# Operand building moved in among the weight-gradient tiles, and dq with ds stationary, in a decode step's backward pass

## The chip, the cores and the metric

One core of a Trainium2 chip runs one program: the forward and backward pass of a four-layer decode step for one token. The metric is the device time of one execution, in microseconds (us). The core has a matrix engine (TensorE, PE in the profile), a vector engine (VectorE, DVE), a scalar engine (ScalarE, ACT) and GpSimd (POOL), each with its own instruction queue; SyncE (SP) only issues transfers here. SBUF is the on-chip memory, PSUM the memory that TensorE writes to, and 16 DMA engines move data to and from device memory (HBM).

## What is computed

The reference runs x = x + A(LN(x)); x = x + B(LN(x)) twice (layers A1, B2, A3, B4) with shared weights, and returns the output and the gradients of all inputs:

```python
def _A_ref(x, k_cache, v_cache, wq, wo):          # x: 1x1x1024, Hq=32, Hkv=4, Dh=128
    W = min(4096, max(256, Sk // 4))              # 4096 of 32768 cached positions
    q = (x @ wq).reshape(B, Sq, Hq, Dh).transpose(0, 2, 1, 3)
    k = jnp.repeat(k_cache[:, :, Sk - W:, :], rep, axis=1)
    v = jnp.repeat(v_cache[:, :, Sk - W:, :], rep, axis=1)
    p = softmax(einsum("bhqd,bhkd->bhqk", q, k) * Dh ** -0.5)
    o = einsum("bhqk,bhkd->bhqd", p, v)
    return o.transpose(0, 2, 1, 3).reshape(B, Sq, Hq * Dh) @ wo
def _B_ref(x, w1, b1, w2):                        # F = 3584
    h = einsum("bsd,df->bsf", x, w1) + b1
    act = h * tanh(softplus(h))                   # mish
    return einsum("bsf,fd->bsd", act, w2)
```

There is one token, so each weight's gradient is a sum of two outer products (one for each layer that uses the weight), and the gradients of the two caches are zero outside the last 4096 positions. Those zeros and the weight gradients are most of what is written.

## The kernel before

All matrix-vector work of one layer is staged behind the loads of its weights. `wq` (`wq_b`), K, V and ten of the sixteen `wo` pieces (`wo_b`) stay in SBUF; w1, w2 and the other six `wo` pieces are loaded again for each pass, in pieces of 448 or 512 KB, into six stream buffers. The order is attention A1 forward, MLP B2 forward, A3 forward, B4 forward and backward in one, `attn_bwd` of A3 (there `first` is true), MLP B2 backward, `attn_bwd` of A1, and then the tail: all weight gradients and the gradients of K and V.

The transfers of zeros (112 of 512 KB) are issued in small groups from POOL's queue (`bg_zeros`, L134) beside the passes, and what is left, 27 of them, from SP's queue in one go (`zeros`, L128) after the last loads of A1's pass. SP's queue is in order: the last `wo` loads, these zeros, a reload of p (L905, `area["p3"]`), then the stores of the tail.

`attn_bwd` (L803) goes through these steps. `T` (L817) transposes a late `wo` piece on TensorE, has it evacuated by ScalarE, and reduces its other half on VectorE; `M` (L826) multiplies. A row pass over the kept `wo` (`drow`) gives the rest of do. `do_p` collects do, two small transposes and products spread it (`dps`, `qps`), and `rows_mm` (L416) computes d = do V^T into two halves `hv` with 32 products, four at a time in column groups of 32. VectorE forms the row sums of p*d (L922) and ds = p*(d - sum) (L933). `half_T` (L431) transposes ds to `dsT`. `cols_mm` (L423) computes dq with 128 products: K is the stationary operand, and 8 columns of `dsT` move. ScalarE scales the result to `dq_bf` (L947). The pass over `wq` (L951) takes 64 products of one broadcast column by 512 into four row strips, `rows_copy` (L242) copies them to SBUF, `rows_sel2` (L251) folds the strips with four fp32 products, and `ln_bwd` (L305) finishes the layer. `warm(n)` (L151) issues n products that nobody reads, between steps. In the A3 pass `fill` (L271) transposes pieces of K, V and wq back beside these steps.

The weight gradients need their operands as rows. These are made by small builds, kept as closures in the list `prep` and issued one at a time by `nextprep` (L1141) at places written by hand inside A1's `attn_bwd`. `spread_rows` (L977: `rows_put`, `tall_left`, `tall_right`) has POOL scatter columns into one of two spread tiles, TensorE transpose up to eight blocks, and ScalarE evacuate them. `row_layout` (L395) takes four products and four masked copies on VectorE (L401). `db1_out` (L1215) writes the gradient of b1.

The tail is a list of jobs, one for each output chunk of [128, 2048] (or 1792), run in order: 14 chunks of dw2 (`dw_tall`), 16 of dw1 (`dw_wide`), 8 of dV (`dkv`), 16 of dwo, 8 of dK, 16 of dwq. A job takes two PSUM tiles of two banks each from the pool `pair` (four such tiles, all of PSUM), fills them with four outer products (eight for dV and dK), evacuates one half at a time, and issues a store from SP; `dkv` stores only after every fourth chunk, two transfers of 1 MB. `ev_out` gives a half to VectorE or ScalarE, whichever has the smaller sum of costs (`evac`, L143: 1.22 against 1.05 a half); other work of VectorE is not counted there.

Of the kernel before, what the change touches and what calls it, by code (L numbers as in the profile page):

```python
# [8 lines left out]
FP32 = mybir.dt.float32  # L9
# [5 lines left out]
P = 128  # L15
HQ = 32
DH = 128
G = 4
# [5 lines left out]
def kernel(  # L24
# [126 lines left out]
    def warm(n):  # L151

        ps = psum1([P, 4, P], FP32, "wps")
        for _ in range(n):
            nc.tensor.matmul(ps, lhsT=ident_bf[:], rhs=ident_bf[:, None, :].to_broadcast([P, 4, P]),  # L155
                             start=True, stop=True, skip_group_check=True)

    def shaped(t, shape):
        n = 1
        for k in shape[1:]:  # L160
            n *= k
        ap = t[0:shape[0], 0:n]
        if len(shape) == 3:
            return ap.rearrange("p (a b) -> p a b", a=shape[1])
        if len(shape) == 4:
            return ap.rearrange("p (a b c) -> p a b c", a=shape[1], b=shape[2])
        return ap

    def psum1(shape, dtype, name):
        return shaped(pt.tile([P, 512 if dtype == FP32 else 1024], dtype, name=name, tag="pt"), shape)  # L170

    def top(kind):
# [12 lines left out]
    def xpose(blocks, dst, how=None, six=False):  # L185

        n = len(blocks)
        pools["turn"] += 1
        if six and pools["turn"] % 6 > 3:
            ps = shaped(pools["top"].tile([P, 1024], BF16, name="tps", tag="h"), [P, 8, P])  # L190
        else:
            ps = psum1([P, 8, P], BF16, "tps")
        for b, ap in enumerate(blocks):
            nc.tensor.transpose(ps[:, b, :], ap, ident_bf[:])  # L194
        evac(dst, ps[:, 0:n, :].rearrange("p b c -> p (b c)"), 0.08 * n + 0.05, 0.11 * n + 0.15, how)

    def nat_blocks(ap2d, nb=8):
        return [ap2d[:, b * P:(b + 1) * P] for b in range(nb)], ap2d
# [106 lines left out]
    def ln_bwd(dn_ps, n32, rstd, g_col, name, nxt):  # L305

        tt = work.tile([P, 2 * TD], FP32, name="tt")
        nc.vector.tensor_copy(tt[:, 0:TD], dn_ps)
        nc.vector.tensor_mul(tt[:, TD:], tt[:, 0:TD], n32[:])
        sps = sm_tile(P, 2 * TD)  # L310
        nc.tensor.matmul(sps[:], lhsT=onesD, rhs=tt[:], start=True, stop=True)
        if nxt == "A1":
            warm(7)
        if nxt == "B2":
            hook("ln")
        ab = work.tile([P, 2], FP32, name="ab")
        nc.vector.reduce_sum(ab[:], sps[:].rearrange("p (a b) -> p a b", a=2), axis=AX.X)
        t2 = work.tile([P, TD], FP32, name="t2")
        nc.vector.scalar_tensor_tensor(out=t2[:], in0=n32[:], scalar=ab[:, 1:2], in1=tt[:, 0:TD],
                                       op0=ALU.mult, op1=ALU.subtract, reverse1=True)  # L320
        gx = work.tile([P, TD], FP32, name="gx")
        nc.vector.tensor_scalar(out=gx[:], in0=t2[:], scalar1=ab[:, 0:1], scalar2=rstd[:, 0:1], op0=ALU.subtract, op1=ALU.mult)
        g_new = keep.tile([P, TD], FP32, name=f"g_{name}")
        nc.vector.tensor_add(g_new[:], g_col[:], gx[:])
        g_bf = pair_col("g" + nxt[0], nxt, TD)
        nc.vector.tensor_copy(g_bf, g_new[:])
        return g_new, g_bf
# [67 lines left out]
    def row_layout(col32, name):  # L395
        x = area[name].rearrange("p (g d) -> p g d", g=G)
        ps = psum1([P, P], FP32, "rps")
        for c in range(NC):
            mm(ps[32 * c:32 * c + 32, 0:P], col32[:], ident_bf[:], True, True, tile_position=(0, 32 * c))
        for g in range(G):  # L400
            nc.vector.tensor_scalar(out=x[:, g, :], in0=ps[:, 0:P], scalar1=gmask[:, g:g + 1], scalar2=None, op0=ALU.mult)  # L401
# [401 lines left out]
    def attn_bwd(g_col, g_bf, lname, sv, first, nxt):  # L803
# [13 lines left out]
        def T(i):  # L817
            c = late[i]
            if c not in held:
                held[c] = wo_load(c)  # L820
            w = held[c]
            xpose(*nat_blocks(w[:, 1, :]), "a")
            nc.vector.tensor_tensor_reduce(out=w[:, 0, :], in0=w[:, 0, :], in1=gbc[:], scale=1.0, scalar=0.0,
                                           op0=ALU.mult, op1=ALU.add, accum_out=wdo[:, i:i + 1])

        def M(i):  # L826
            c = late[i]
# [21 lines left out]
        if not first:  # L849
            after_do()  # L850
            prep.extend([
                lambda: tall_left("w2", "a", 0),
                lambda: tall_left("w2", "a", 1),
                lambda: tall_right("w2", "gB"),
                lambda: rows_put(area["R1"], 0, "nB", "rep"),
                lambda: rows_put(area["R1"], 1, "dh", "pieces"),
                lambda: row_layout(sA3["dorep"], "do3"),
                lambda: row_layout(sA3["qrep"], "q3"),
            ])

        for i in range(2, len(late) + 1):
# [16 lines left out]
        if first:  # L878
            fill(1, ["K", "wq"], "a")
        else:  # L880
            warm(4)
        dps = psum1([HQ, P], BF16, "dps")
        nc.tensor.transpose(dps[:, 0:P], do_p[:].rearrange("p t c -> p (t c)"), ident_bf[:])
        dr = work.tile([HQ, P, 2], BF16, name="dr", tag="rw5", padded_shape=[HQ, P, 2])
# [8 lines left out]
        for e in range(2):  # L893
            mm(qps[:, :, e], drf[:, e * P:(e + 1) * P], fold16[:], e == 0, e == 1)
        if not first:
            warm(2)
        sv["dorep"] = pad_cols(pad, qps[:].rearrange("p c e -> p (c e)"), 1.0, f"do_{lname}")
        top("halves")
        hv = halves("d")
# [1 line left out]
        if first:  # L901
            fill(3, ["K", "wq"], "a")
        else:
            after_v()
            nc.sync.dma_start(area["p3"], out_5[0:P, :])  # L905
            prep.extend([
                lambda: tall_left("wo", "o", 0),
                lambda: tall_left("wo", "o", 1),
                lambda: tall_right("wo", "gA"),
                lambda: rows_put(area["Rq"], 0, "nA", "rep"),  # L910
                lambda: row_layout(sA1["dorep"], "do1"),
                lambda: row_layout(sA1["qrep"], "q1"),
                db1_out,
            ])
            nextprep(2)
            warm(3)
        scr = work.tile([P, WC], BF16, name="scr", tag="kp")
        sdp = work.tile([P, 2], FP32, name="sdp")
# [8 lines left out]
        nc.vector.tensor_copy(sd[:], lps[:])  # L927
        ds = sv["p"] if first else area["ds"]
        dsT = work.tile([P, TJ, P], BF16, name="dsT", tag="kp")
        qacc = acc_tile(HQ)  # L930
        for hf in range(2):
            hs = slice(hf * 512, (hf + 1) * 512)
            nc.vector.scalar_tensor_tensor(out=ds[:, hs], in0=hv[hf][:], scalar=sd[:, 0:1], in1=sv["p"][:, hs], op0=ALU.subtract, op1=ALU.mult)  # L933
# [1 line left out]
        if first:  # L935
            fill(100, ["K"], "a")
        else:
            nextprep(1)
            warm(3)
        for hf in range(2):  # L940
            half_T(ds, dsT, hf, "va"[hf])
        if not first:
            nextprep(1)
        for hf in range(2):
            cols_mm(qacc, dsT, kv["K"], hf)
        dq_bf = pair_col("dq", lname, HQ)
        nc.scalar.activation(dq_bf, qacc[:], ACT.Copy, scale=scale)  # L947
        if first:
# [2 lines left out]
        for h in range(HQ):  # L951
            for half in range(2):
                row_mm(nrow, 2 * half + h % 2, dq_bf[:, h:h + 1],
                       wq_b[:, 4 * half:4 * half + 4, h // 16, (h % 16) * P:(h % 16 + 1) * P], h < 2, h >= HQ - 2)
            if not first and h % 6 == 5:
                nextprep()
        nps = sm_tile(P, TD)
        yr = rows_copy(nrow, "v")
        if first:
            hook("copy")  # L960
        else:
            rows_put(area["Rq"], 1, "dq", "heads")
        rows_sel2(yr, Cols8(nps, True))
        if first:
            hook("sel")
# [11 lines left out]
    def spread_rows(n, put, dst):  # L977

        sp = area["spread"][pools["sturn"] % 2]
        pools["sturn"] += 1  # L980
        for l in range(2):
            put(sp.rearrange("p j (q x) -> p j q x", q=4), l)
        ps = psum1([P, 8, P], BF16, "rw")
        for j in range(n):
            nc.tensor.transpose(ps[:, j, :], sp[:, j, :], ident_bf[:])
        evac(dst, ps[:, 0:n, :].rearrange("p j x -> p (j x)"), 0.69, 1.0, "a")

    def rows_put(R, side, kind, how):

# [19 lines left out]
    def tall_left(nm, kind, half):  # L1009

        src = pairs[kind]
        nb = src.shape[2] // 2
        lo, n = 8 * half, min(8, nb - 8 * half)

        def put(spread, l):
            c = src[:, l, 2 * lo:2 * (lo + n)].rearrange("p (c t) -> p c t", t=2)
            for tt in range(2):
                nc.gpsimd.tensor_copy(spread[:, 0:n, 2 * tt:2 * tt + 2, l], c[:, :, tt:tt + 1].to_broadcast([P, n, 2]))

        spread_rows(n, put, tall[nm][:, lo * P:(lo + n) * P])  # L1020
# [120 lines left out]
    def nextprep(n=1):  # L1141
        for _ in range(min(n, len(prep))):
            prep.pop(0)()
# [80 lines left out]

    g0, g0b = attn_bwd(g1, g1b, "A1", sA1, False, "X0")
    level()
    nextprep(100)
    col_out(g0b, TD, out_1[0, 0, :])
    top(None)
    pacc.release()  # L1230
# [4 lines left out]
        return area[nm].rearrange("p (g d) -> p g d", g=G)  # L1235

    slots.extend(wq_t)
    dkv(area["p3"], r3("do3"), sA1["p"], r3("do1"), out_3)
    dw_tall("wo", HQ, out_5.rearrange("(c p t) d -> c p t d", p=P, t=2))
    dkv(sA3["ds"], r3("q3"), sA1["ds"], r3("q1"), out_2)  # L1240
    dw_wide(lambda: area["Rq"], 512, 2048, False, out_4)
    run(1000)
    zeros(1000)
    assert not zero_jobs
# [30 lines left out]
```

## Time and profile before

| | us |
|---|---|
| median of 8 runs | 450.67 (446.31 to 453.22) |
| the profiled execution, its own time | 451.45 |
| its span in the profile | 449.6 |
| busy PE / PEld / DVE / ACT / POOL | 325.8 / 220.5 / 235.4 / 225.0 / 63.9 |
| moved by DMA | 171.20 MB, mean 381 GB/s |
| last loads issued, last zeros issued by SP | 294.6, 330.4 |
| first evacuation of a dW chunk, its store issued | 344.65, 346.00 |

PEld is the load of a stationary operand. A row of the timeline gives the start, the length, the engine, the source line, what is written and read, the number of instructions, and in brackets how long the engine had been idle and who released it. Many rows carry L230, L194 or L149 because small helpers issue most matmuls, transposes and copies; they are told apart by the names of the tiles: `acc<-dsT,K` is dq, `acc<-wq_b,dq_pair` the pass over wq, `d` the product with V, `kps` the transposes of ds, `rw` the transposes of operand rows, `rps` the row layouts, `wps` warm-ups, `ops` the outer products of the tail.

### The profile page before, as it was taken

How to read it: one execution, taken by the hardware profiler on the slowest of the kernel's cores; microseconds unless marked ns; L12 is line 12 of the kernel's file. 1: busy time of each engine (PE TensorE's matmuls, PEld its weight loads, DVE VectorE, ACT ScalarE, POOL GpSimd, SP SyncE). 2: the span in 40 equal slices, each digit the busy share in tenths (PEclk: the TensorE clock that was granted, in tenths of full speed). 3: DMA queues.
4: the chain of work that ended last, by engine and by line, in shares of the span. 5: the costliest groups of instructions: out<-in, count | busy, mean ns of one | idle time of the engine just before them, and what ended most of it. 6: DMA issues, size and time to landing. Idle time of an engine off the chain costs nothing.

```text
span 449.6 us, 12085 instructions
## 1 busy us (share of the span) xinstructions
PE 325.8 (72%) x5180; PEld 220.5 (49%) x5180; DVE 235.4 (52%) x484; ACT 225.0 (50%) x262; POOL 63.9 (14%) x165
## 2 busy tenths in 40 slices
PE   0465856497988798977899579796775857989720
PEld 0233515496466798964897579764532111112100
DVE  3124201196333476782265765463415978999930
ACT  1122100075153486875693355427214988998930
POOL 2000000011332122251341102015001000000000
PEclk9999555576879899998799668969867555555555
DMA  8999999999999999999999999999992999899998
GB/s 318 374 414 417 407 408 375 408 367 360 405 414 374 396 330 383 368 402 417 414 414 394 361 367 343 408 393 412 414 399 82 403 404 403 334 406 400 407 406 326
DMA packets 52049, 171.20 MB, mean 381 GB/s; under 512 B 5184, under 2 KB 12380, under 8 KB 50972
## 3 DMA queue, kind: packets, MB, share of 16 engines
q1 hardware_dynamic: 39536, 125.58, 72.3%
q0 software_dynamic: 12416, 44.84, 25.2%
q8 instruction: 40, 0.66, 0.6%
q14 instruction: 13, 0.11, 0.1%
q10 hardware_dynamic: 44, 0.01, 0.0%
HBM read 71.58 MB, written 98.84 MB: 379 GB/s over the span
## 4 chain that ended last, share of the span: by engine, by line
PE 23%; ACT 15%; DMA 6%; issue 5%; DVE 3%; POOL 1%; DVEq 0%; ACTq 0%; SPq 0%; POOLq 0%
PE ops L230 7%; DMA w_c<-in_B_w_dram 6%; PE tps L194 6%; ACT wq_b L149 5%; PE acc L230 3%; ACT K L149 3%; ACT wo_b L149 2%; ACT st_o L149 2%; PE wps L155 1%; ACT V L149 1%; PE sm L230 1%; PE d L230 1%; ACT wo_c L149 1%; PE tps L628 1%; DVE K L146 1%
## 5 line engine op out<-in xcount | busy, mean ns | idle before, releaser
L139 POOL DMA_DIRECT2D out_dram<-zt x85 | 45.5, 538 | 45.5 <-DMA out_dram<-zt 40.3
L230 PEld LDWEIGHTS <-w_c 128*128 128x128 bf16 x1120 | 37.3, 102 | 22.2 <-DMA w_c<-in_B_w_dram 16.8
L638 ACT COPY w_c<-tps 128x1024 bf16<-128x1024 bf16 x28 | 28.3, 1012 | 27.1 <-PE tps L628 19.8
L652 DVE CUSTOM_DVE_ANT_0 scr<-w_c,gbc 128x1024 bf16<-128x1024 bf16 x28 | 34.2, 1221 | 9.2 <-DMA w_c<-in_B_w_dram 7.9
L230 PE MATMUL ops<-V 2*128 2x512 bf16 (+1 forms) x160 | 34.4, 599 | 5.8 <-ACT wq_b L149 2.8
L149 ACT COPY K<-tps 128x1024 bf16<-128x1024 bf16 x20 | 19.4, 1031 | 29.9 <-PE tps L194 29.9
L146 DVE CAST wq_b<-ops 128x1024 bf16<-128x1024 f32 (+1 forms) x29 | 31.7, 1151 | 3.6 <-PE ops L230 3.1
L230 PEld LDWEIGHTS <-V 128*128 128x128 bf16 (+2 forms) x448 | 15.9, 101 | 35.4 <-issue 35.2
L149 ACT CAST wq_b<-ops 128x1024 bf16<-128x1024 f32 (+1 forms) x31 | 31.7, 1137 | 2.2 <-PE ops L230 2.0
L230 PE MATMUL ops<-wo_b 2*128 2x512 bf16 x120 | 23.3, 567 | 10.9 <-ACT wq_b L149 6.6
L628 PE MATMUL tps<-ident_bf,w_c 128*128 128x128 bf16 x224 | 23.9, 273 | 0.8 <-DMA w_c<-in_B_w_dram 0.8
L230 PE MATMUL q<-wq_b,nA_pair 128*32 128x512 bf16 x128 | 11.5, 440 | 16.5 <-DMA wq_b<-in_A_wq_dram 16.5
L149 ACT COPY w_b<-tps 128x1024 bf16<-128x1024 bf16 x20 | 19.5, 1015 | 6.1 <-PE tps L194 6.1
L146 DVE COPY K<-tps 128x1024 bf16<-128x1024 bf16 x12 | 8.1, 690 | 25.3 <-PE tps L194 23.4
L230 PE MATMUL acc<-a_pair,w_c 128*128 128x16 bf16 x448 | 15.8, 173 | 7.5 <-DMA w_c<-in_B_w_dram 7.5
L230 PEld LDWEIGHTS <-wo_b 2*128 2x128 bf16 (+1 forms) x184 | 6.6, 100 | 29.3 <-issue 28.7
L194 PE MATMUL tps<-ident_bf,w_c 128*128 128x128 bf16 x224 | 16.5, 231 | 3.4 <-DMA w_c<-in_B_w_dram 3.4
L149 ACT CAST K<-ops 128x1024 bf16<-128x1024 f32 x18 | 17.5, 1014 | 2.6 <-PE ops L230 2.1
L628 PEld LDWEIGHTS <-w_c 128*128 128x128 bf16 x224 | 18.1, 123 | 1.3 <-DMA w_c<-in_B_w_dram 0.9
L149 ACT COPY w_c<-tps 128x768 bf16<-128x768 bf16 (+1 forms) x14 | 11.6, 830 | 14.2 <-PE tps L194 14.2
L194 PE MATMUL tps<-ident_bf,K 128*128 128x128 bf16 x256 | 18.3, 227 | 0.2 <-ACT K L149 0.2
L146 DVE COPY w_c<-tps 128x1024 bf16<-128x1024 bf16 (+1 forms) x18 | 11.7, 661 | 12.0 <-PE tps L194 8.6
(322 smaller groups left out, 668.8 us busy)
## 6 DMA issues: line engine op xcount, KB each, us to landing
out_dram<-zt POOLq DMA_DIRECT2D x85, 512.0 KB, 10.5
w_c<-in_B_w_dram SPq DMA_DIRECT2D x32, 448.0 KB, 6.2
w_c<-in_B_w_dram SPq DMA_DIRECT2D x28, 512.0 KB, 7.2
out_dram<-zt SPq DMA_DIRECT2D x27, 512.0 KB, 10.8
wo_c<-in_A_wo_dram SPq DMA_DIRECT2D x24, 512.0 KB, 8.5
wq_b<-in_A_wq_dram SPq DMA_DIRECT2D x16, 512.0 KB, 11.3
out_dram<-K SPq DMA_DIRECT2D x8, 1024.0 KB, 10.2
out_dram<-wq_b SPq DMA_DIRECT2D x16, 512.0 KB, 9.9
```

Of the source, the lines that this page charges most:

```text
L139: nc.gpsimd.dma_start(zero_jobs.pop(0), zt[:])
L146: nc.vector.tensor_copy(out_ap, in_ap)
L149: nc.scalar.copy(out_ap, in_ap)
L155: nc.tensor.matmul(ps, lhsT=ident_bf[:], rhs=ident_bf[:, None, :].to_broadcast([P, 4, P]), start=True, stop=True, skip_group_check=True)
L194: nc.tensor.transpose(ps[:, b, :], ap, ident_bf[:])
L230: nc.tensor.matmul(out_ap, lhsT=lhsT, rhs=rhs, start=start, stop=stop, skip_group_check=True, **kw)
L628: nc.tensor.transpose(self.ps[c][:, b, :], w[:, 1, b * P:(b + 1) * P], ident_bf[:])
L638: nc.scalar.copy(self.w[c][:, 1, :], self.ps.pop(c)[:].rearrange("p b c -> p (b c)"))
L652: nc.vector.tensor_tensor_reduce(out=scr[:], in0=w[:, 0, :], in1=gbc[:], scale=1.0, scalar=0.0, op0=ALU.mult, op1=ALU.add, accum_out=self. ...
```

## The change

There are four edits. First, dq: the transposed ds is now the stationary operand (32 columns), and 512 columns of K move; four such products run in column groups, over eight j, into `qrow` [128, 512]. VectorE copies it to SBUF, and four fp32 products with the constant `fold` pick each head's group and add the four strips. Both passes do so. Second, ten operand builds (four row layouts, five operands for dwo and dwq, and `db1_out`) leave A1's `attn_bwd` and are inserted into the job list of the tail, at positions 5, 9, ... 41; there they take their PSUM tile from `pair`, and their evacuation goes to the engine with the smaller sum. Third, the jobs are woven: after dw2, two dw1 chunks to one dV chunk, then two dwo to one dK, then dwq. Fourth, in the do part of `attn_bwd` all six reductions are issued ahead, the last two transposes are evacuated by VectorE, and warm-ups are changed; in A3's pass two fills of wq move ahead of the fold.

```diff
     def psum1(shape, dtype, name):
+        if "pair" in pools:
+            return shaped(pools["pair"].tile([P, 1024 if dtype == FP32 else 2048], dtype, name=name, tag="pair"), shape)
...
         if nxt == "A1":
-            warm(7)
+            warm(5)
...
-            xpose(*nat_blocks(w[:, 1, :]), "a")
-            nc.vector.tensor_tensor_reduce(out=w[:, 0, :], in0=w[:, 0, :], in1=gbc[:], scale=1.0, scalar=0.0,
-                                           op0=ALU.mult, op1=ALU.add, accum_out=wdo[:, i:i + 1])
+            if not first and i == len(late) - 1:
+                warm(2)
+            if i == 0:
+                for k, c in enumerate(late):
+                    nc.vector.tensor_tensor_reduce(out=held[c][:, 0, :], in0=held[c][:, 0, :], in1=gbc[:], scale=1.0, scalar=0.0,
+                                                   op0=ALU.mult, op1=ALU.add, accum_out=wdo[:, k:k + 1])
+            xpose(*nat_blocks(w[:, 1, :]), "a" if i < 4 else "v")
...
-                lambda: row_layout(sA3["dorep"], "do3"),
-                lambda: row_layout(sA3["qrep"], "q3"),
...
-            warm(4)
+            warm(1)
         dps = psum1([HQ, P], BF16, "dps")
...
         if not first:
-            warm(2)
+            warm(1)
         sv["dorep"] = pad_cols(pad, qps[:].rearrange("p c e -> p (c e)"), 1.0, f"do_{lname}")
...
-            prep.extend([
-                lambda: tall_left("wo", "o", 0),
-                lambda: tall_left("wo", "o", 1),
-                lambda: tall_right("wo", "gA"),
-                lambda: rows_put(area["Rq"], 0, "nA", "rep"),
-                lambda: row_layout(sA1["dorep"], "do1"),
-                lambda: row_layout(sA1["qrep"], "q1"),
-                db1_out,
-            ])
-            nextprep(2)
+            nextprep(100)
             warm(3)
...
-        qacc = acc_tile(HQ)
+        qrow = acc_tile(512)
...
-            nextprep(1)
-            warm(3)
+            warm(4)
         for hf in range(2):
             half_T(ds, dsT, hf, "va"[hf])
-        if not first:
-            nextprep(1)
-        for hf in range(2):
-            cols_mm(qacc, dsT, kv["K"], hf)
+        for j in range(TJ):
+            for c in range(NC):
+                mm(qrow[32 * c:32 * c + 32, :], dsT[:, j, 32 * c:32 * c + 32], kv["K"][:, :, 4 * j + c, :],
+                   j == 0, j == TJ - 1, tile_position=(0, 32 * c))
+        yq = rows_copy(qrow, "v")
+        if first:
+            fill(2, ["wq"], "a")
+        else:
+            warm(3)
+        qacc = sm_tile(P, HQ)
+        for g in range(G):
+            mm(qacc[:, 8 * g:8 * g + 8], yq[:, g * P:(g + 1) * P], fold[:, 8 * g:8 * g + 8], g == 0, True)
...
-            if not first and h % 6 == 5:
-                nextprep()
...
-        else:
-            rows_put(area["Rq"], 1, "dq", "heads")
...
-        evac(dst, ps[:, 0:n, :].rearrange("p j x -> p (j x)"), 0.69, 1.0, "a")
+        evac(dst, ps[:, 0:n, :].rearrange("p j x -> p (j x)"), 0.69, 1.0, None if "pair" in pools else "a")
...
-    nextprep(100)
...
+    def weave(a, b):
+        while a or b:
+            jobs.extend(a[0:2])
+            jobs.extend(b[0:1])
+            del a[0:2], b[0:1]
...
+    jobs.extend(stage["w"][:n2])
+    weave(stage["w"][n2:], stage["v"])
+    weave(stage["o"], stage["k"])
+    jobs.extend(stage["q"])
+    for k, f in enumerate(late_prep):
+        jobs.insert(5 + 4 * k, f)
     run(1000)
```

Here `stage` holds the jobs by output (w: dw2 and dw1, v: dV, o: dwo, k: dK, q: dwq), n2 is 14, and `late_prep` lists the builds in this order: layouts do3 and do1, the two halves of the left operand of dwo and its right one, layouts q3 and q1, the two sides of dwq's operand (nA, dq), and db1.

More of the change, by code (lines that the diff above doesn't have):

```diff
@@ L1237, with take @@
     slots.extend(wq_t)
+    stage = {}
+    def take(nm):
+        stage[nm] = jobs[:]
+        del jobs[:]
+    take("w")
     dkv(area["p3"], r3("do3"), sA1["p"], r3("do1"), out_3)
+    take("v")
     dw_tall("wo", HQ, out_5.rearrange("(c p t) d -> c p t d", p=P, t=2))
+    take("o")
     dkv(sA3["ds"], r3("q3"), sA1["ds"], r3("q1"), out_2)
+    take("k")
     dw_wide(lambda: area["Rq"], 512, 2048, False, out_4)
+    take("q")
+    late_prep = [
+        lambda: row_layout(sA3["dorep"], "do3"),
+        lambda: row_layout(sA1["dorep"], "do1"),
+        lambda: tall_left("wo", "o", 0),
+        lambda: tall_left("wo", "o", 1),
+        lambda: tall_right("wo", "gA"),
+        lambda: row_layout(sA3["qrep"], "q3"),
+        lambda: row_layout(sA1["qrep"], "q1"),
+        lambda: rows_put(area["Rq"], 0, "nA", "rep"),
+        lambda: rows_put(area["Rq"], 1, "dq", "heads"),
+        db1_out,
+    ]
+    def weave(a, b):
[3 more added lines that the diff above has]
+            del a[0:2], b[0:1]
+    n2 = NW2
+    jobs.extend(stage["w"][:n2])
[4 more added lines that the diff above has]
+        jobs.insert(5 + 4 * k, f)
     run(1000)
```

## The prediction

> **What bounds the kernel now.** I read the page's slices first (DMA is the mean busy share of the 16 DMA engines, in tenths; PEclk the granted TensorE clock).
>
> ```profile
> PEclk9999555576879899998799668969867555555555
> DMA  8999999999999999999999999999992999899998
> GB/s 318 374 414 417 407 408 375 408 367 360 405 414 374 396 330 383 368 402 417 414 414 394 361 367 343 408 393 412 414 399 82 403 404 403 334 406 400 407 406 326
> ```
>
> The DMA engines are full almost throughout, whatever the compute engines do. Only moved bytes or filled holes can change the time, and this change moves no byte. The holes are the slice of 82 GB/s (near 340 us), a shallow one nine slices from the end, and the ends. So next I read busy times by stretch, of the tail (columns: stretch, length, PE, PEld, DVE, ACT, POOL busy with counts, clock, DMA share, GB/s).
>
> ```profile
> 301.00:321.00 20.00, 14.00 (x236) 8.86 (x234) 10.17 (x30) 9.69 (x13) 6.44 (x31) 1.00 1.03 414
> ...
> 328.00:335.00 7.00, 5.68 (x55) 2.29 (x58) 0.00 (x0) 1.60 (x2) 0.00 (x0) 0.51 1.03 413
> ...
> 337.00:347.00 10.00, 4.96 (x39) 2.58 (x40) 5.42 (x17) 3.36 (x4) 1.68 (x6) 0.74 0.10 39
> 347.00:361.00 14.00, 11.02 (x54) 2.21 (x52) 13.81 (x14) 13.85 (x15) 0.00 (x0) 0.50 1.02 404
> 361.00:378.00 17.00, 10.09 (x56) 1.91 (x56) 13.60 (x14) 14.92 (x15) 0.00 (x0) 0.50 1.02 404
> 378.00:389.00 11.00, 10.27 (x72) 2.05 (x70) 10.04 (x10) 9.96 (x11) 0.00 (x0) 0.50 0.85 334
> 383.00:385.00 2.00, 1.97 (x18) 0.46 (x16) 1.28 (x3) 1.84 (x3) 0.00 (x0) 0.50 0.18 62
> ```
>
> Until 337 the zero stores (27 on SP's queue behind the last weight loads) keep the DMA full. From 337 to 347 only a tenth is used: **9.0 us lost**, since the first dW tile is not ready. At 383 to 385 another **1.65 us** is lost: dV chunks store only after every fourth. After 385 the DMA is full to 447.4, where the last store ends; 2.2 us of span follow.
>
> Third, the chain of waits up to the first dW evacuation at 344.65 (start, length, what):
>
> ```profile
> 311.68 0.36 PE acc L230 x8
> ...
> 312.50 0.86 PE wps L155 x4
> ...
> 316.93 2.16 DVE wo_b L401 x8
> 319.09 0.59 DVE scr L922
> ...
> 324.73 13.82 issue
> ...
> 339.07 0.53 POOL wo_b L998 x3
> 339.61 0.05 issue
> 339.65 0.62 PE rw L985 x8
> 340.27 0.86 PE sm L230 x8
> ```
>
> The row operands sit on it: eight mask products (L401) ahead of the softmax sums, and the dq operand (L998, L985) ahead of the fold. The 13.82 us of "issue" is the chain passing through POOL; the timeline shows what PE did then:
>
> ```profile
> 323.62 3.46 PE L230 MATMUL acc<-dsT,K 128*128 128x8 bf16 x128
> 327.36 0.39 PE L230 MATMUL acc<-wq_b,dq_pair 128*32 128x512 bf16 x1 [0.29 <-ACT dq_pair L947]
> 329.32 1.47 PE L230 MATMUL acc<-wq_b,dq_pair 128*32 128x512 bf16 x11 [1.57 <-issue]
> ...
> 338.19 0.67 DVE L246 COPY yr<-acc 128x512 f32<-128x512 f32 x1
> ```
>
> The 64 products of the wq pass take 10.8 us (327.36 to 338.15), with a stall, five operand builds between them and half the clock; the same 64 in the A3 pass took 3.64 (234.81 to 238.45).
>
> **The change, part by part, in the A1 chain.** Savings against 344.65:
> 1. LayerNorm warm-ups 7 to 5, at 0.45 each: 0 to 0.9, as the row copy beside them ends earlier; 0.4.
> 2. Two of six wo transposes evacuated by DVE (0.69) not ACT (1.02): ACT's queue between 303.4 and 311.6 loses 2.0, but the operand builds and their four PSUM tiles pace it too; 0.8 (0 to 2.0). DVE's six reductions now run ahead, 6 x 1.15 = 6.9 us to about 306, when DVE idles until 312 today; do_p waits for no more.
> 3. Warm-ups 4 to 1 and 2 to 1, at 0.21: 0.65 + 0.2, ending where do_p is ready.
> 4. Row layouts gone from L401: 2.16, and the first half-sum starts when its half of d (1.84 for both) is done: 2.5 in all.
> 5. Transposes ahead of and behind kps (0.55 and 0.87) gone, one warm-up added: 0.3 + 0.8.
> 6. The new dq. Out: 128 products, 3.46. In: 32 products of 128x32 by 512 in four column groups; the nearest row is d, the same shape, 32 in 1.84. Then a copy of 0.67 (row L246) and a fold of four fp32 products like L256's, 0.86. The sum is 3.37 plus a semaphore step or two: **the new dq saves nothing** (-0.4 to +0.2; I take 0). The Trainium skill speaks against it (TensorEngine Tiling (Array Packing), section PSUM Bottleneck: tiling speeds the products, not the evacuation). By TensorE: Matmul & The Clock Gate (Measured speedup vs the span model) three column tiles gain 2.38x: on some 216 ns a product that is 32 x 91 = 2.9 us, an estimate, and dq would lose 1.1. The d row's 58 ns a product is nearer; I take the row.
> 7. The wq pass without builds: 3.64 at full clock, 7.8 at half (12 in 1.47 after 331), plus perhaps the 1.6 stall, which I can't tie to a build. Saves 3.0 to 7.2; I take 3.64 + 1.6, so 5.6. The clock decides. The rule (same page, HAM oscillation) is that gaps over about 3.4 us re-throttle; here PE sat 2.06 us idle for L401 and the clock fell at 321.5. By rule or row, step 4 removes that gap, so fewer warm-ups should not cost the clock.
> 8. The dq operand leaves the way from yr (ends 338.86) to the fold (340.27): 1.3.
>
> Sum 0.4+0.8+0.85+2.5+1.1+0+5.6+1.3 = 12.55: first evacuation S at **332.1** (330.0 to 336.5), first dW store 1.35 later, before the zeros end at 337.5. The 9.0 hole closes. SP's queue keeps its order (zeros, p3, dW stores), so the dW stores queue behind the zeros, unhurt. POOL now has out_1's small store ahead of the o operand copies; those are first needed some 14 us later.
>
> **What comes due next.** From S to the end of dV (388.65) takes 44.0 us today, for 14 w2, 16 w1 and 8 dV chunks; from there stores last 58.7 to 447.4, a DMA-full stretch. The change puts ten builds into those 44 us (positions 5 to 41 of the job list: 14 plain jobs, then two w1 to one dV). DVE pays, in the built order: 16 mask products x 0.27 (2.16 for eight) = 4.3, db1's three ops 0.67, three of five operand evacuations 0.69+0.69+0.42 = 1.8, in all 6.8 us; ACT two at 0.93, 1.9. DVE's busy time in the 44 us is 39.4, ACT's 40.7, so DVE needs 46.2 with no idle at all. PE adds transposes (8 at 0.11 cold, 0.9 us a build), and each build takes one of four PSUM pairs. The balance of copies does not count the mask products. Half of DVE's idle 4.6 may stay: 48.5, a price of **4.5** (2.2 to 16.7, below). Mixing dV's PE-bound chunks (1.17 us of PE each, 10.3 of 11 us) with w1 should pay part; its stores come later, but no byte does. Weaving wo and dK behind that is DMA-full already: 0, as long as stores are queued.
>
> Last store: 332.1 + 44.0 + 4.5 + 58.7 = 439.3; plus 2.2 a span of 441.5 against 449.6, **8.1 less**. The profiled execution took 451.45, 1.85 over its span; I carry the difference to the median, 450.67 - 8.1 = **442.6**.
>
> The A3 pass gets the same dq, and its fills move. I cost it at nothing: POOL keeps issuing zeros until 239.7 and six w2 loads stand queued, so the DMA stays full (share 1.03 at 230 to 240). Without that cover it would be the 0.4 of step 6 and a queue's 0.9 ACT copy or two.
>
> **Cases.**
> - A, 0.58: hole closed, copies due next. Own range 440 to 446.7 (S 330.0 to 334.7, price 2.2 to 6, not under B's floor).
> - B, 0.17: weaving pays for the builds and the DMA stays full from 337.5. Floor: 347.0 to 447.4 less 1.65 is 98.75, so 436.25 + 2.2 = 438.5, 11.1 less, 439.6. For it: DVE and ACT idle in the w1 stretch. Against: 46.2 of DVE work from 332.1 ends at 378.3 and 58.7 more is 437.0 only without idle.
> - C, 0.15: clock stays half and the stall stays, S = 336, builds cost 7: 445.7 + 2.2 = 447.9, median 449.0. For it: half clock at 328 to 335 today.
> - D, 0.10, slower: builds run serially, each holding the copying engines up for its whole latency, since PSUM has four pairs and a job takes two. Four layouts at 1.6 (products 0.45, masks 1.08), five operands at 1.8 (transposes 0.9, copy up to 1.0), db1 1.3: 16.7 in place of 4.5, so 453.7, median 454.8. It turns into a loss from a price over 332.1 + 44 + 58.7 = 434.8 to 447.4, 12.6 us. Against: POOL prepares rows ahead, and copies of two chunks overlap a build.
> - That the new dq does not speed dq at all I hold likely (step 6), without effect on these sums.
>
> Within 0.5% (448.4 to 452.9, about what this measurement can tell) lies most of C. Faster: A, B and a quarter of C, 0.79; same 0.11; slower D, 0.10. The range 438.8 to 450.5 leaves out D and the edges of B and C.
>
> **What would show it.** DMA share near 1.0 at 337 to 347; first dW evacuation at 330 to 336; no L401 or rw instructions between d and the wq pass, which takes 4 to 6 us; dq's new matmuls near 1.9 and the path from dsT to dq_pair near 3.9; in the woven stretch DVE over 90% busy and some DMA slack before dV's first stores. Wrong if the clock is half in the wq pass, if PE waits for copies around each build, or if DMA holes of more than 5 us open in the woven stretch.

## The result, and the profile after

The changed kernel took 447.09 us (median of 21 runs, 444.02 to 449.76) against 450.21 for the kernel before (58 runs). The ratio is **0.994 (95% interval 0.9921 to 0.9959)**: 3.1 us less, a gain that is real and small. The forecast was 8.1 us less. The measured time lies in the range given, but the gain is less than half of what was forecast.

The profiled execution of the changed kernel has a span of 443.3 us, 6.3 less than that of before. The two traces overstate the gain, since one is of a quick execution and the other of a long one, so there is a second trace of each kernel below; the traces of e3_old_dq, e6_move_only, e7_no_psum and e9_counted are of executions 2 to 5 us above the medians of their kernels, so that only lengths and clocks of single stages are taken from them.

The slices of the page, as shown of the kernel before:

```profile
PEclk9998655575888899999999668998975555555555
DMA  8999999999999999999999999999999969899997
GB/s 316 388 409 419 405 408 392 407 371 376 385 416 389 395 348 363 386 392 378 417 415 403 350 395 384 375 364 414 416 415 410 417 258 397 331 407 405 403 406 315
```

The slice of 82 GB/s is gone. In its place stand two shallower dents, 258 and 331 GB/s, further to the right. The busy times of stretches of the tail show where they lie (stretch, length, busy PE, PEld, DVE, ACT, POOL with counts, clock, DMA share, GB/s):

```profile
337.00:347.00 10.00, 6.69 (x43) 2.30 (x43) 8.84 (x13) 7.75 (x9) 0.65 (x4) 0.50 1.03 419
347.00:356.00 9.00, 7.05 (x42) 1.76 (x39) 6.37 (x7) 7.14 (x7) 1.12 (x6) 0.50 1.02 414
356.00:369.00 13.00, 10.41 (x66) 2.64 (x64) 11.95 (x18) 9.82 (x9) 0.00 (x0) 0.50 0.69 275
369.00:376.00 7.00, 4.97 (x38) 1.75 (x35) 5.37 (x8) 5.51 (x7) 0.07 (x1) 0.50 1.02 403
376.00:385.00 9.00, 6.46 (x46) 1.43 (x42) 8.22 (x8) 8.79 (x9) 0.46 (x1) 0.50 0.80 316
385.00:440.00 55.00, 34.41 (x176) 7.99 (x173) 40.33 (x36) 38.56 (x41) 0.00 (x0) 0.50 1.02 405
```

At 337 to 347 the DMA engines are full: the hole of the kernel before is closed. At 356 to 369 and 376 to 385, ahead of the two groups of dV stores, they wait again: the engines that fill the stores are still busy with dw1, dV and operand builds. Added up over one-microsecond windows (those with a share under 0.95), the holes between 330 and the last store are 5.8 us, against 10.8 before.

The chain of waits of the changed kernel through the A1 pass (start, length, what):

```profile
308.54 0.36 PE acc L232 x8
...
310.99 1.91 PE d L232 x32
...
314.01 0.17 DVE sd L922
...
316.07 1.87 PE acc L232 x32
...
318.02 0.70 DVE yr L248
...
318.77 1.07 PE sm L232 x8
...
320.11 3.67 PE acc L232 x64
...
323.80 0.70 DVE yr L248
...
324.55 1.07 PE sm L232 x8
```

From d on, no operand build stands on it any more. From d to the sums is 3.0 us (5.7 before), and the wq pass is one piece of 3.67 us at full clock (10.8 before). The new dq is the three rows 316.07, 318.02 and 318.77: the products take 1.87, and the copy and the fold as long again. The first dW evacuation, S, is at 329.04 (344.65 before). That is in time: the last zeros are issued at 328.6, and in the kernel before the DMA stayed full for some 7 us after that point (330.4 to 337.5).

### The profile page after: what moved, and what is told of

It reads as the page before. It is cut to its first block, busy times and chain, and to the rows that moved or that the text cites. A ratio compares the mean times of both kernels' runs of the same rounds, so it can differ in the third digit from the quotient of the medians.

```text
span 443.3 us, 11728 instructions
## 1 busy us (share of the span) xinstructions
PE 321.6 (73%) x5004; PEld 215.6 (49%) x5004; DVE 240.8 (54%) x492; ACT 220.6 (50%) x256; POOL 63.7 (14%) x165
## 4 chain that ended last, share of the span: by engine, by line
PE 22%; ACT 14%; DMA 7%; DVE 6%; issue 3%; POOL 1%; DVEq 0%; ACTq 0%; SPq 0%
DMA w_c<-in_B_w_dram 7%; PE tps L196 6%; PE ops L232 5%; ACT wq_b L149 5%; PE acc L232 5%; ACT K L149 2%; PE sm L232 2%; ACT wo_b L149 2%; ACT st_o L149 2%; ACT V L149 2%; PE rw L983 2%; DVE K L146 1%; PE d L232 1%; DVE st_o L146 1%; DVE wq_b L146 1%
## 5 line engine op out<-in xcount | busy, mean ns | idle before, releaser
L232 PEld LDWEIGHTS <-w_c 128*128 128x128 bf16 x1120 | 37.4, 102 | 23.9 <-DMA w_c<-in_B_w_dram 18.1
L232 PEld LDWEIGHTS <-V 128*128 128x128 bf16 (+2 forms) x448 | 17.2, 102 | 37.5 <-issue 37.2
L149 ACT CAST wq_b<-ops 128x1024 bf16<-128x1024 f32 (+1 forms) x32 | 33.4, 1121 | 3.8 <-PE ops L232 3.4
L146 DVE CAST wq_b<-ops 128x1024 bf16<-128x1024 f32 (+1 forms) x28 | 30.5, 1146 | 1.1 <-PE ops L232 1.0
L146 DVE CAST K<-ops 128x1024 bf16<-128x1024 f32 x16 | 19.6, 1224 | 6.2 <-PE ops L232 6.2
L248 DVE COPY yr<-acc 128x512 f32<-128x512 f32 x6 | 4.2, 692 | 30.1 <-PE acc L232 30.1
L149 ACT CAST K<-ops 128x1024 bf16<-128x1024 f32 x16 | 16.2, 1012 | 5.1 <-PE ops L232 5.1
L146 DVE COPY w_c<-tps 128x1024 bf16<-128x1024 bf16 (+1 forms) x18 | 11.7, 661 | 12.3 <-PE tps L196 10.1
```

What stands on the lines that cost most here:

```text
L146: nc.vector.tensor_copy(out_ap, in_ap)
L149: nc.scalar.copy(out_ap, in_ap)
L232: nc.tensor.matmul(out_ap, lhsT=lhsT, rhs=rhs, start=start, stop=stop, skip_group_check=True, **kw)
L248: nc.vector.tensor_copy(yr[:], bank[:])
```

## The experiments

Positions in a trace vary from run to run by some us, because the stage before varies. So two lengths are read from each trace: from SP's first zero store to S (the chain; 49.97 before, 35.70 after), and from S to the issue of the second group of dV's stores (the woven stretch: 53.8 after, some 44.3 before; the last dV copy ends within 0.3 us of it). The chain itself is not steady: in the nine traces whose A1 code is that of the changed kernel it is 34.94 to 38.05 long. All ratios are to the kernel before on the same chip.

**e1_again and e10_before_again: a second trace of each kernel, unchanged.**

> The changed kernel once more, for a second trace. In its first trace the first dW evacuation came at 329.04 (S), dV ended 53.7 us later (44.0 before), and the DMA holes in the woven stretch summed to 5.8 us; the pair of traces differed by 6.3 us, the medians by 3.1. Theory 1 (the price of the woven builds is fixed work, the traces differ from the medians by chance): S within 1.5 us of 329, S to end of dV 52.5 to 55, holes 5 to 8, ratio 0.992 to 0.996. Theory 2 (the first trace caught a good phase of the TensorE clock in the A1 chain): S at 331 to 336 with half clock in the wq pass, holes 7 to 11.

> The kernel before once more, for a second trace. The pair of traces differed by 6.3 us, the medians by 3.1; the second trace of the changed kernel had a span of 444.9. If the first trace of before was a bad one in the A1 chain (S 344.65, wq pass 10.8 us with a stall of 1.6): S at 341 to 343.5, wq pass 7 to 9.5, hole 6 to 8 us. If the chain is always so long: S at 344 or more, hole 9 us.

The changed kernel: median 447.34, ratio 0.9944 (0.9921 to 0.9967); span 444.9, S at 330.58, wq pass 3.64 at full clock, woven stretch 53.8, holes 6.0 us. So theory 1, with S at the edge of its band: the price of the woven stretch is the same to a tenth. The kernel before: span 447.1, S at 342.07, wq pass 325.23 to 335.3 (10.1 us, longer than the 7 to 9.5 expected) with the stall of 1.5 us at the same place, holes 6.2 + 1.8 = 8.0 us. Of its second trace, the two holes (the second stretch is the wait for dV's stores):

```profile
337.00:345.00 8.00, 4.81 (x37) 2.52 (x38) 4.45 (x11) 3.94 (x5) 0.52 (x2) 0.58 0.22 86
380.00:383.00 3.00, 2.82 (x20) 0.46 (x16) 2.28 (x3) 2.83 (x4) 0.00 (x0) 0.50 0.41 157
```

The trace that I had worked from was the longer one. The means of two traces, holes of 9.4 before and 5.9 after, differ by 3.5 us: that is enough for the 3.1 us of the medians.

**e4_no_builds: what the builds cost.**

```diff
-    for k, f in enumerate(late_prep):
-        jobs.insert(5 + 4 * k, f)
+    jobs.append(late_prep[-1])
```

> The changed kernel without nine of the ten builds in the tail (dwo, dwq, dK, dV are formed from what lies in their operand areas), db1 at the very end. Theory A (builds are the price): S to end of dV falls from 53.7 to 43 to 46, holes under 1 us, 4 to 6 us faster than the changed kernel. Theory B (the weave is the price): S to end of dV 49 or more, holes 3 us or more, at most 3 us faster.

Median 440.09 (4 runs), ratio 0.981 (0.9746 to 0.9874). The woven stretch is 41.8 us. From S to the last dV copy, first the changed kernel, then this one:

```profile
329.04:382.78 53.74, 38.69 (x238) 10.57 (x234) 46.44 (x59) 43.57 (x43) 3.56 (x20) 0.50 0.91 364
```

```profile
331.85:373.57 41.72, 33.63 (x184) 7.51 (x180) 39.48 (x38) 40.47 (x40) 0.06 (x1) 0.50 1.03 410
```

The third and fourth busy times are DVE and ACT. Without builds DVE idles 2.2 us of 41.7, and the DMA share is full. With them DVE works 7.0 us more, but the stretch is **12.0 us longer**, and DVE idles 7.3 us. Theory A holds (the stretch is even shorter than its 43 to 46) and B falls: woven jobs alone are quicker than the 44.0 us of the old order, by 2.3.

**e2_plain: the old order of jobs, with the builds.**

```diff
-    weave(stage["w"][n2:], stage["v"])
-    weave(stage["o"], stage["k"])
+    jobs.extend(stage["w"][n2:] + stage["v"])
+    jobs.extend(stage["o"] + stage["k"])
```

> The changed kernel with the jobs in the old order (dw2, dw1, dV, dwo, dK, dwq), builds at the same list positions 5 to 41. Theory A (the builds are the price: each takes one of four PSUM pairs and passes TensorE and a copying engine in series): S to end of dV stays 52 to 55, holes 5 to 8 and mostly at dV, time within 1.5 us of the changed kernel. Theory B (the weave is the price: eight-product dV chunks between dw1 chunks break the pipelining): S to end of dV falls to 47 to 50, holes 2 to 4, 2 to 4 us faster than the changed kernel. Rival C (the weave is what paid): 2 us or more slower, since all eight dV chunks come with no store after each.

Median 448.78, ratio 0.9968 (0.9945 to 0.9991); the woven kernel on the same chip had 0.9944. The second group of dV's stores is issued some 54 us after S, and 7.7 us of holes gather at 366 to 381, ahead of dV's first stores. Theory A again: without the weave the stretch is no shorter. In the plain order the builds cost 54.1 less 44.0, so 10.1: the 2.3 us that the weave gains without builds are nearly gone with them. That the weave helps by 1.4 us here is inside the intervals.

**e6_move_only: the kernel before with the builds in the tail and the weave, nothing else.**

The edit is the second and third of the change; dq, the reductions and the warm-ups stay as before.

> The kernel before with only the second and third edits: the ten builds in the tail and the woven jobs; old dq, old order of reductions, old warm-ups. Theory (closing the hole is paid back by the builds): S at 334 to 338, S to end of dV 53 to 55, then the end at S + 53.8 + 58.3 + 2.25, which is 448.5 to 452; ratio 0.996 to 1.006. Rival (the move alone is what paid): ratio 0.990 to 0.995.

Median 449.18 (22 runs), ratio 0.9988 (0.9964 to 1.0012): no gain that can be told. The chain is 38.9 us, so the move alone takes 8.4 to 11 us off it (47.35 and 49.97 in the two traces before); the woven stretch is 53.8 and pays it back. The theory holds, and the rival (0.990 to 0.995) falls. So the moved builds alone do not make the gain of the whole change (0.994). It takes the new dq, the order of the reductions and the warm-ups as well, and what each of these brings was not separated.

**e7_no_psum and e8_no_layouts: what the 12 us are made of.** In the first, the builds of the tail keep their POOL scatters and their copies but read SBUF; in the second the four row layouts are left out.

```diff
-        ps = psum1([P, P], FP32, "rps")
-        for c in range(NC):
-            mm(ps[32 * c:32 * c + 32, 0:P], col32[:], ident_bf[:], True, True, tile_position=(0, 32 * c))
         for g in range(G):
-            nc.vector.tensor_scalar(out=x[:, g, :], in0=ps[:, 0:P], scalar1=gmask[:, g:g + 1], scalar2=None, op0=ALU.mult)
+            nc.vector.tensor_scalar(out=x[:, g, :], in0=ident_f[:, 0:P], scalar1=gmask[:, g:g + 1], scalar2=None, op0=ALU.mult)
...
-        ps = psum1([P, 8, P], BF16, "rw")
-        for j in range(n):
-            nc.tensor.transpose(ps[:, j, :], sp[:, j, :], ident_bf[:])
+        ps = sp
+        if "pair" not in pools:
+            ps = psum1([P, 8, P], BF16, "rw")
+            for j in range(n):
+                nc.tensor.transpose(ps[:, j, :], sp[:, j, :], ident_bf[:])
```

> The changed kernel with its nine operand builds in the tail cut to their copying halves: the same POOL scatters, mask products and evacuating copies on the same engines, but read from SBUF, with no TensorE product, transpose or PSUM tile (so dwo, dwq, dK and dV are not formed from the right rows). Theory A (the price comes from the pass through TensorE and one of four PSUM pairs, which makes each build serial): S to end of dV falls from 53.8 to 43 to 47 and the time by 4 us or more. Theory B (it is the copying engines' added work, some 6.8 us on VectorE): S to end of dV 49 or more, at most 3 us faster.

```diff
     for k, f in enumerate(late_prep):
-        jobs.insert(5 + 4 * k, f)
+        if k not in (0, 1, 5, 6):
+            jobs.insert(5 + 4 * k, f)
```

> The changed kernel without the four row layouts in the tail (dK and dV are formed from what lies there); five operand builds and db1 stay. Without nine builds S to end of dV fell by 12.0. If each build costs its serial latency, layouts 1.1 to 1.4 and operands 1.2 to 1.6 each: S to end of dV 48 to 49.5. If the mask products, which the balance of copies does not count, carry most of it: 44 to 46. If the transposes carry most: 51 or more.

Without TensorE and PSUM the woven stretch is 48.4 us: 5.4 of the 12.0 gone, between the two theories. (Four mask products from SBUF took 0.87 us against 1.12 from PSUM, so 1.0 of the 5.4 is that.) So 4.4 to 5.4 us are the pass through TensorE and PSUM, which e7 takes away together, so that the products and the scarce pairs are not told apart; 6.6 us and more stay with POOL and the copying engines. Without layouts the stretch is 47.0, in none of the three bands: four layouts cost 6.8, **1.7 each**, more than the 1.1 to 1.4 expected; five operands and db1 cost 5.2, 0.87 each, less than the 1.2 to 1.6 expected. The ratios were 0.9776 and 0.981 with intervals about 0.005 to each side, from four runs each, which can't tell the two apart. Nor is e4_no_builds (0.981) quicker than e8, though its stretch is 5.2 us shorter: neither trace has a hole between 330 and its last store, and with the DMA full the shorter stretch brought nothing that these runs can tell. The chain of the changed kernel shows how a layout (`rps`) and an operand (`rw`) hold it up:

```profile
359.90 1.04 PE ops L232 x6
360.94 0.23 PE rps L232 x4
361.16 0.56 PE ops L232 x2
361.74 2.46 ACT wq_b L149 x2
364.20 0.04 issue
364.25 1.04 PE ops L232 x6
365.28 0.97 PE rw L983 x8
366.25 0.60 PE ops L232 x2
366.85 2.44 ACT wq_b L149 x2
```

Matrix engine and copies take turns: products of a dV chunk, products of a build, products of the next chunk, and only then two copies, which must end before the pairs for the next dV chunk are free. With four PSUM pairs, of which a job takes two and a build one, little can run ahead.

**e9_counted: VectorE's mask products counted in the balance of copies.**

```diff
+        if "pair" in pools:
+            ev[0] += 1.12
         for g in range(G):
             nc.vector.tensor_scalar(out=x[:, g, :], in0=ps[:, 0:P], scalar1=gmask[:, g:g + 1], scalar2=None, op0=ALU.mult)
```

> The changed kernel, with 1.12 us added to VectorE's sum in the balance of copies for each row layout built in the tail, so that later halves go to ScalarE instead. Leaving the four layouts out shortened S to end of dV by 6.8, 1.7 each. If that is because their VectorE time is not counted (VectorE takes its full share of copies besides): S to end of dV falls from 53.8 to 50 to 52, 1.5 to 3 us faster than the changed kernel. If it is the serial pass through TensorE, PSUM pair and four mask products: 53 to 55, time within 1 us.

Woven stretch 52.0, 1.8 shorter; median 445.58, ratio 0.9903 (0.9867 to 0.9938). So the missing count is 1.8 of the layouts' 6.8; the other 5.0, 1.25 for each, stay with the serial pass and the work itself. As a time it is not separable from the changed kernel (0.9944 on another chip).

**e3_old_dq and e11_old_dq_wide: the old dq in the changed kernel.** In the second, one 512-column warm-up follows every 16 of its products in the A1 pass.

```diff
-        for j in range(TJ):
-            for c in range(NC):
-                mm(qrow[32 * c:32 * c + 32, :], dsT[:, j, 32 * c:32 * c + 32], kv["K"][:, :, 4 * j + c, :],
-                   j == 0, j == TJ - 1, tile_position=(0, 32 * c))
-        yq = rows_copy(qrow, "v")
         if first:
             fill(2, ["wq"], "a")
-        else:
-            warm(3)
-        qacc = sm_tile(P, HQ)
-        for g in range(G):
-            mm(qacc[:, 8 * g:8 * g + 8], yq[:, g * P:(g + 1) * P], fold[:, 8 * g:8 * g + 8], g == 0, True)
+        for hf in range(2):
+            cols_mm(qacc, dsT, kv["K"], hf)
```

> The changed kernel with the old dq (K stationary, 128 products, no copy and no fold) in both attention passes. If the new dq saves nothing by itself (step 6 of the prediction): from dsT to dq_pair 3.5 to 4.0 us as against some 3.8, S within 0.5 us, time within 1 us of the changed kernel. If the new dq was a real gain: S 1.5 us later or more and the time up by as much.

> The changed kernel with the old dq (128 products with 8 columns moving) and, in the A1 pass, one 512-column warm-up product after every 16 of them. In all seven traces with the new dq the wq pass took 3.64 us at full clock; with the old dq it took 5.49, 6.57 and 10.8. If narrow products let the clock fall and wide ones hold it: the wq pass takes 3.6 to 3.8. If the clock falls for another reason (the phase of a window, the operand's layout): 5 us or more. S follows: dq is 1.7 longer by the added products.

With the old dq, from the end of kps to the wq pass is 3.56 us; with the new one 4.03. So the new dq is slower by 0.5 where it stands. But after the old dq the wq pass takes 5.49 us in place of 3.64. The two together make S 1.4 us later, between the two cases expected. (In the trace of e3_old_dq the chain is 39.23, 3.5 longer than in that of the changed kernel; 2.4 of that lie ahead of the transposes of ds, where e4 and e7, with the new dq, lost as much.) PE's rows of e3_old_dq:

```profile
320.00 3.34 PE L232 MATMUL acc<-dsT,K 128*128 128x8 bf16 x128
323.64 5.49 PE L232 MATMUL acc<-wq_b,dq_pair 128*32 128x512 bf16 x64 [0.29 <-ACT dq_pair L941]
```

and two stretches from each trace, the dq and the six microseconds after it, whose granted clock is the third number from the end. First e3_old_dq, then e11_old_dq_wide:

```profile
319.00:323.00 4.00, 3.72 (x128) 3.50 (x129) 0.95 (x2) 0.58 (x1) 0.00 (x0) 1.00 1.03 417
323.00:329.00 6.00, 5.58 (x78) 2.32 (x75) 0.00 (x0) 0.20 (x1) 0.00 (x0) 0.72 1.02 414
```

```profile
319.00:323.00 4.00, 3.95 (x103) 2.85 (x103) 0.00 (x0) 0.20 (x1) 0.00 (x0) 1.00 1.02 411
323.00:329.00 6.00, 4.45 (x68) 2.47 (x60) 0.92 (x3) 0.00 (x0) 0.00 (x0) 1.00 1.03 417
```

PE is busy for nearly all of both dq stretches, by count of instructions even more so in the first. Yet after 128 products of 8 columns the clock falls, and with eight wide products among them it stays at 1.00; the wq pass is then 3.8 us of products with one gap of 0.4. In all four traces with the plain old dq (both of before, move_only, e3_old_dq) the wq pass of A1 ran partly or wholly at half clock; in all nine with the new dq it took 3.64 at full clock. In the A3 pass, where transposes follow, plain narrow products ran in five traces (in that of e11_old_dq_wide too, whose wide ones are in A1 only). The clock fell in three, both of before and move_only, and stayed in e3_old_dq and e11_old_dq_wide: narrow products make the fall likely, and what stands near them counts too. As a time, e3_old_dq gave 448.22, ratio 0.9965 (0.9934 to 0.9995), 0.9 above e1_again and not separable from it; e11_old_dq_wide gave 449.19, ratio 1.0002 (0.9965 to 1.0039), which is more than its trace explains (span 446.1, holes 7.7); I leave that open.

**e5_spread and e12_spread_counted: builds where stores are queued.**

```diff
-    n2 = NW2
-    jobs.extend(stage["w"][:n2])
-    weave(stage["w"][n2:], stage["v"])
-    weave(stage["o"], stage["k"])
-    jobs.extend(stage["q"])
-    for k, f in enumerate(late_prep):
-        jobs.insert(5 + 4 * k, f)
+    jobs.extend(stage["w"])
+    weave(stage["o"], stage["v"])
+    weave(stage["q"], stage["k"])
+    order = {13: 0, 16: 1, 19: 2, 22: 3, 25: 4, 42: 5, 45: 6, 48: 7, 51: 8, 60: 9}
+    for at in sorted(order, reverse=True):
+        jobs.insert(at, late_prep[order[at]])
```

The second has the line of e9_counted besides.

> The changed kernel with another job order: dw2, dw1, then two dwo chunks to one dV, then two dwq to one dK; five builds (do3, do1, the dwo operands) fall among the later dw1 chunks, the other five behind the middle of dwo. Theory (the builds and the store-less dV chunks cost time only where no stores are queued, and a queue builds up over 30 plain chunks): DMA holes after 330 below 2 us, 5 to 7 us faster than the changed kernel, ratio to before 0.975 to 0.985. Rival (the price of the builds is paid wherever they stand): within 2 us of the changed kernel.

> The spread job order (dw2, dw1, dwo with dV, dwq with dK; builds where stores are queued), with the layouts counted in the balance of copies. The spread order had a ratio of 0.984 and only one hole of 1.2 us after 330, so little is left: ratio 0.980 to 0.986, the same as without the count within 0.4%.

e5_spread: median 443.01, ratio **0.984 (0.9804 to 0.9875)**; holes after 330 of 1.3 us. e12_spread_counted: median 442.68, ratio **0.9833 (0.9794 to 0.9873)**, and no hole at all from 337 to its last store:

```profile
337.00:347.00 10.00, 8.26 (x44) 1.91 (x40) 10.00 (x11) 9.74 (x11) 0.00 (x0) 0.50 1.03 411
347.00:438.00 91.00, 63.33 (x370) 16.37 (x367) 73.54 (x80) 70.84 (x73) 2.28 (x11) 0.50 1.02 406
```

Both beat both kernels. The work is the same. Five builds now stand among the dw1 chunks and five from the middle of dwo on, and the dV chunks, which store only after every fourth, come behind 30 chunks that each bring a store. Both were moved at once, so what each is worth is not shown. The count made no difference here, as expected.

## Why the prediction was right in its mechanism and wrong in its size

- **The bound and the hole.** Right: bytes and holes set the time, and the hole at 337 closes. The traces' holes (9.4 to 5.9) are enough for the medians' difference.
- **Steps 1 to 8, the chain.** Forecast 12.55; the traces' chains fell from 47.35 and 49.97 to 35.7 and 35.95, so 11.4 to 14.3. By step in the two first traces, forecast and found: LayerNorm 0.4 and 1.2; the two transposes 0.8 and 0.6; warm-ups 0.85 and 0.84; layouts off the sums 2.5 and 2.7; around kps and dq 1.1 and 0.6; wq pass 5.6 and 7.1; dq operand 1.3 and 1.26.
- **Step 6, the new dq.** "Saves nothing" is right for its own path, where it lost 0.5 (forecast -0.4 to +0.2); the row of d (1.84) gave the products' 1.87, not the 2.9 us estimated from the page's ratio. Not seen: with the wide products the clock stays up for the next pass, which is worth 1.9 us and more there.
- **Step 7, the clock.** The full clock came, the stall did not, and the reason was wrong, so that the value taken, 3.64 plus the stall, was near by luck. I gave the 2.06 us of idleness, and its removal by step 4, as what decides the clock. But e3_old_dq has no such gap ahead of dq and still loses the clock, and the second trace of before has the gap and keeps it, up to the end of dq:

```profile
318.32 0.24 PE L230 MATMUL sm<-sdp,fold 128*32 128x1 f32 x8 [2.06 <-DVE sdp L922]
```

```profile
317.75:321.17 3.42, 2.22 (x36) 1.47 (x37) 3.02 (x8) 1.01 (x1) 0.60 (x4) 1.00 1.03 417
321.17:324.58 3.41, 3.41 (x131) 3.41 (x129) 0.01 (x1) 1.50 (x2) 0.47 (x2) 1.00 1.03 416
324.58:331.41 6.83, 5.05 (x50) 2.08 (x47) 0.00 (x0) 0.78 (x2) 0.00 (x0) 0.50 1.03 412
```

In the first trace the clock that fell at 321.3 was back at 324.7, and the wq pass ran into a second fall, at 328.1, behind dq. With the old dq and no builds in it, the pass took 5.49 and 6.57 (e3_old_dq and move_only), which saves 5.3 and 4.2 of the 10.8, not 5.6.

- **The step that failed: the price of the builds** in "What comes due next", 4.5 us, measured 9.7 (53.7 less 44.0), with the weave's own gain of 2.3 us in it, so 12.0 for the builds. The sum of VectorE's work was right (46.2 forecast with no idle, 46.44 found). The error is the idle time put on top: I took half of the old 4.6 and found 7.3. A build passes TensorE, a PSUM pair and a copying engine in turn: with TensorE and PSUM left out (e7) the idle time of VectorE is 4.3, and the stretch is 48.4, near the 48.5 forecast, though with the weave's 2.3 in it. That is the mechanism of case D in part, at 12.0 in place of its 16.7: for layouts it fits (1.7 against 1.6 each) only because 0.45 of each is the missing count of e9, and for operands it is too dear (0.87 against 1.8). With 9.7 in the sum, 332.1 + 44.0 + 9.7 + 58.7 + 2.2 = 446.7, 2.9 less than 449.6. That this meets the measured 3.1 so well is luck in part: S came 1.5 to 3.1 us earlier than 332.1, and 449.6 is the longer of the two spans before (447.1 the other).
- **The weave behind dV** cost nothing, as forecast: the DMA is full from 385 on. What I called a wrong sign, "DMA holes of more than 5 us open in the woven stretch", is what came: 5.8 and 6.0; and VectorE was busy for 86% of that stretch, not over 90%.

## What to carry to other kernels

Where stores bound the tail, the price of side work among output tiles depends on whether stores are queued when it comes: the same builds and chunks took 4 us less in an order that lets a queue form first. A small build that takes a scarce PSUM buffer and passes two engines can cost more than its busy time (12.0 us of stretch for 7.0 of VectorE); bound it by its busy time and its latency. Work moved off one chain must be priced on the chain it lands in, and the traces of two executions of one kernel can differ by nearly as much as the change (spans 449.6 and 447.1).

## What the runs showed of the hardware that was not expected

128 back-to-back products of 8 columns kept PE busy in the records (3.72 of 4 us) and the granted clock still fell to half at or after them, in four A1 passes of four (three A3 passes of five); the same products with one of 512 columns after every 16 kept it at 1.00, in the one trace taken. In all fourteen traces the changes of the granted clock lie 3.41 us or whole multiples of it apart. In the second trace of before, shown above, PE was busy for all of the last such step ahead of the fall, 321.17 to 324.58, with transposes of an operand at its start and narrow products from 321.58 on. The two steps of e11_old_dq_wide that hold its dq were about as busy, and the clock stayed:

```profile
317.18:320.59 3.41, 3.41 (x92) 2.76 (x93) 0.21 (x1) 0.59 (x1) 0.00 (x0) 1.00 1.03 416
320.59:324.00 3.41, 3.20 (x72) 1.93 (x71) 0.00 (x0) 0.20 (x1) 0.00 (x0) 1.00 1.03 411
```

How the products lie to these steps may be why the A3 pass kept its clock in two traces; that was not tried. The gap of 1.5 to 1.6 us after the first product of the wq pass came in both traces of the kernel before, with no releaser in the records, and not in move_only, where the operand builds are gone from that pass; so it seems to come with the builds, and how was not tried.
